# Sparse attention and GELU layers on one core: an earlier request for the last batch's queries and keys, and new instruction orders in five of eight halves

## The chip, the cores and the metric

The kernel runs on one core of a Trainium2 chip. The metric is the device time of one execution in microseconds (us). Five engines run in parallel, each through its own list of instructions in order: TensorE (PE for its matmuls, PEld for its weight loads), VectorE (DVE), ScalarE (ACT), GpSimd (POOL), and SyncE (SP), which here only issues transfers. Semaphores let one engine wait for another.

## The reference

Block-sparse attention on 4 batches of 8 heads with 768 tokens of 64 values, and then two layers with an exact GELU between them. A block is 32 tokens; a block of queries sees itself, its neighbours, the first and the last block, and three sampled blocks. The first and last block of queries see everything.

```
scores = scale * np.matmul(q, k.transpose(0, 1, 3, 2))
mask = np.abs(blk_i - blk_j) <= window
mask = mask | (blk_i == 0) | (blk_j == 0) | (blk_i == n_blocks - 1) | (blk_j == n_blocks - 1)
for qb in range(n_blocks):
    for kb in sampled_blocks[qb]:
        mask[qb * block:(qb + 1) * block, kb * block:(kb + 1) * block] = True
...
attn = np.exp(scores)
attn = attn / (np.sum(attn, axis=-1, keepdims=True) + 1e-09)
return np.matmul(attn, v).astype(np.float32)
...
h = x @ w_in
g = 0.5 * h * (1.0 + erf(h * inv_sqrt2))
return (g @ w_out).astype(np.float32)
```

x is the attention's output as 3072 rows of 512; w_in is 512 x 2048 and w_out 2048 x 512.

## The kernel before, in words

**Halves.** Each batch is worked in two halves of 384 tokens (`units`, L336), eight in all. The first half of a batch is dense: it also holds the two blocks of queries that see everything. The second is not. For each half, in order, comes its attention, then its first layer, and then its second layer, which is mixed into the attention of the next half.

**The attention of a half** works in rounds. A round is a score tile in PSUM, of two blocks of queries (four activations) or, in a dense round, of one of the two full blocks for half of the heads. `scores` (L347) makes the products on TensorE, `maxima` (L376) the negated row maxima on DVE (`nm`), `exponentials` (L389) the exponentials on ACT (`pp`), and `turned` (L408) transposes them on DVE (`pT`, or `ptd` for a dense round). When the rounds of a group are through, `values` (L429) makes the products with the values on TensorE (`av`; L442 is the dense one of 96 products, L481 the others of 104, or 92 for a group of three blocks), `divided` (L491) divides on DVE (`den`, `rec`, `xh`), and `outputs` (L508) turns the result on TensorE (`tx`) and copies it with ACT into `xT`, the first layer's input. PSUM has three score-sized tiles (`psA`), which scores, values and the first layer share, and two single banks that the second layer's sums and the turns use in alternation.

**The first layer** (`ffn1_step`, L547) is 64 products from `xT` (`hp`, L536), and ACT's GELU of them (`g`). **The second layer** (`ffn2_pieces`, L572) is 48 products (`op`, L579) in three sums of 16, each then copied by ACT (`os`, L563) and stored by SP (L565).

**The order of the work** is written out by hand. `manual_schedule` (L58) leaves each engine's list as the program writes it, and `attention` (L612) writes a half by a string of words, `PLANS` (L744): `s`, `m`, `e`, `t` with a number are scores, maximum, exponential and transpose of that round; `w`, `d`, `o` with a letter are values, division and output of a group (`d` the dense one; `O` copies the output in two pieces); `f` with a number is that many of the second layer's products; `S` asks for finished sums to be stored; `G` loads ACT's table for the GELU; `x` calls a function by name. Since each engine has its own list, a word places an instruction only among those of the same engine. The second half of a batch also holds, as its last two rounds, the first two dense rounds of the next batch (`ahead`), so that in the fourth half s6 and m6 belong to the third batch's first dense round. That half's words put s7 and m7 ahead of s6 and m6.

**Queries and keys.** From the third batch on they come by token: `load_by_token` (L123) issues six transfers of 128 KB from POOL for the queries into `qn`, and six for the keys into `kn`. Then `turn_queries` (L135) has SP issue one transposing transfer from `qn` into the batch's turned queries, and `turn_keys` (L132) one from `kn` a half later. POOL and SP take what they issue in order. `hold_loads` (L170) is a copy of one element on POOL (`mark`, L172) that waits for the value that it reads: what stands behind it on POOL isn't issued earlier. In the loop over the halves (L765), before the change, the hold and the loads of both the third and the fourth batch stand behind the first step of a first layer (L784 to L789). For the fourth, the last, that is the first layer of the fourth half, and the value held on is the half's second output copy in `xT`. Behind these loads on POOL stand another hold and the copies of sampled blocks into `gb` (L807, L808) for the fifth half.

Of the kernel before, what the change touches and what calls it, by code (L numbers as in the profile page):

```python
# [20 lines left out]
def kernel(  # L21
# [12 lines left out]
    B, H, S, D = q.shape  # L34
# [42 lines left out]
    kn = const.tile([P, H, PI * D], BF16, name="kn")  # L77
    qn = const.tile([P, H, PI * D], BF16, name="qn")
# [91 lines left out]
    def hold_loads(x):  # L170

        nc.gpsimd.tensor_copy(mark, x)  # L172
# [166 lines left out]
    column = {}  # L339
    for n, unit in enumerate(units):  # L340
        for t, quad in enumerate(unit.quads):
            for i in range(4):
                column[unit.b, 4 * quad + i] = (xTs[n % 2], P * t + BL * i)

    st = {}

    def scores(unit, *rnds):  # L347
# [28 lines left out]
    def maxima(rnd):  # L376
        A = st[rnd, "A"]
        nm = small.tile([P, 4], F32, name="nm")
        if rnd[0] == "s":
            n = len(rnd[1])  # L380
            A4 = A.rearrange("p (g j c) -> p g j c", g=2, j=2)
            nc.vector.tensor_reduce(out=nm[:, 0:2 * n].rearrange("p (g j) -> p g j", g=2),  # L382
                                    in_=A4[:, :, 0:n, :], op=ALU.max, axis=AX.X, negate=True)
        else:
            nc.vector.tensor_reduce(out=nm[:, 0:1], in_=A[:, 0:S], op=ALU.max, axis=AX.X,  # L385
                                    negate=True)
        st[rnd, "nm"] = nm

    def exponentials(rnd):  # L389
        A, nm = st.pop((rnd, "A")), st.pop((rnd, "nm"))  # L390
# [349 lines left out]
    def next_keys(b):  # L740
# [22 lines left out]
    }  # L763

    for n, unit in enumerate(units):  # L765
        nxt = units[n + 1] if n + 1 < len(units) else None
        b = unit.b
# [9 lines left out]
        for s in range(KOUT // 2):  # L777
            ffn1_step(n, 2 * s)
            if s == 0:
                if n == 0:  # L780
                    hold_loads(sampled(nxt.place[J1[7]], NR - 1)[0:1, BW - 1:BW])
                    gather(nxt, J1[8:], others, engine=nc.gpsimd)
                    ones(1)
                elif fresh and b + 2 < B:  # L784
                    xT, t0 = column[b, unit.groups[-2][0]]
                    hold_loads(xT[0:1, 0, t0:t0 + 1])
                    load_by_token(qn, q, b + 2)
                    load_by_token(kn, k, b + 2)
                    turn_queries(b + 2)  # L789
                elif nxt is not None and not fresh:  # L790
                    if b + 1 < B:
                        turn_keys()
                        hold_loads(sampled(nxt.place[J1[7]], NR - 1)[0:1, BW - 1:BW])
                        load_values(b + 1)
                    else:
                        gather(nxt, J1[8:], others, engine=nc.gpsimd)
            if s == 7 and nxt is not None:
                table(AF.Exp)
                if n > 0 and not fresh and b + 1 < B:
                    next_keys(b + 1)  # L800
                    hold_loads(keys(b + 1)[0:1, NB, 0:1])
                    gather(nxt, J1[8:], others, engine=nc.gpsimd)
            if fresh and s == 0:
                gather_fixed(keys(b + 1), nxt.place)
                gather(nxt, J0[3:9], known)
                gather(nxt, J0[:3], known)
                hold_loads(sampled(nxt.place[J0[2]], NR - 1)[0:1, BW - 1:BW])  # L807
                gather(nxt, J0[9:], others, engine=nc.gpsimd)  # L808
        filler = ffn2_pieces(n)
# [8 lines left out]
            attention(nxt, filler, PLANS[1], extra | {"v": later_values, "s": partial(spare_key, keys(1))},  # L818
                      ahead=units[n + 2])
        else:  # L820
            attention(nxt, filler, PLANS[n + 1], ahead=units[n + 2] if not fresh and b + 1 < B else None)


# [28 lines left out]
```

## Time and profile before

| | us |
|---|---|
| median of 3 runs | 274.39 (273.89 to 275.86) |
| the profiled execution | 274.32 |
| its span, first to last instruction | 272.5 |
| TensorE busy in the span | 252.6 |
| attention of the third to eighth half (with the second layer of the half before) | 19.67, 17.77, 21.56, 17.86, 19.44, 17.15 |
| the first layer between them | 10.4 each |

The granted clock of TensorE was 1.00 throughout. The chain of work that ended last runs for 82% of the span through PE and for 7% through ACT. In the views, a line of the timeline gives start, length, engine, source line and operation, out<-in and the number of instructions merged; in brackets stands the idle time of that engine just before, with what ended it, where "issue" means that the profile shows nothing that the engine waited for. In the DMA views q0 holds the transfers that POOL issues, q1 those that SP issues, and q8 the fetching of instructions; the columns are packets, MB, and the time that the packets took as a share of 16 engines over the window.

### The profile page before, as it was taken

Reading aid. Unit: us, or ns where it says so; the run is one execution under the profiler, and the core shown is the slowest. Engines: PE = TensorE matmul, PEld = TensorE weight load, DVE = VectorE, ACT = ScalarE, POOL = GpSimd, SP = SyncE. Lnnn points to the kernel's source line nnn. Section 1 sums busy time; section 2 is a strip of 40 time slices with the busy share of each in tenths; the row PEclk is TensorE's granted clock in tenths of the full one; section 3 lists DMA queues with packets and bytes.
Section 4 is the critical chain, followed back from the end, with each engine's and each line's share of the span. In section 5 each row is a group of like instructions: output and inputs, shape, how many; then the busy total and the mean of one; then the engine's idle time right before and its main releaser. Section 6 shows DMA issues by size and latency. Waiting matters only on the chain.

```text
span 272.5 us, 11555 instructions
## 1 busy us (share of the span) xinstructions
PE 252.6 (93%) x4944; PEld 144.1 (53%) x4944; DVE 203.3 (75%) x472; ACT 206.7 (76%) x381; POOL 103.6 (38%) x212
## 2 busy tenths in 40 slices
PE   0899679999999999999999799999999999999994
PEld 0634455455664656545554466455655655465543
DVE  7499659599897988699989686698869892981000
ACT  8789655977869975897779755995889956986611
POOL 7799960735964000940991002920040160000000
PEclk9999999999999999999999999999999999999999
DMA  6999399979999117921999017911101110021012
GB/s 96 186 191 149 55 147 202 206 123 143 93 172 129 43 41 158 104 28 68 98 156 172 8 41 156 117 43 44 38 1 43 43 41 0 5 79 41 0 38 82
DMA packets 75910, 24.41 MB, mean 90 GB/s; under 512 B 65489, under 2 KB 72914, under 8 KB 75858
## 3 DMA queue, kind: packets, MB, share of 16 engines
q0 software_dynamic: 57440, 13.64, 53.4%
q1 hardware_dynamic: 18418, 10.03, 15.5%
q8 instruction: 39, 0.64, 1.0%
q14 instruction: 13, 0.11, 0.1%
HBM read 27.26 MB, written 6.29 MB: 123 GB/s over the span
## 4 chain that ended last, share of the span: by engine, by line
PE 82%; ACT 7%; issue 3%; DMA 3%; DVE 3%; POOL 1%; POOLq 0%; ACTq 0%
PE hp L536 30%; PE op L579 26%; PE av L481 10%; PE sc L356 6%; DMA qn<-in_q_dram 3%; PE tx L513 2%; PE op L608 2%; ACT pp L399 2%; PE av L442 2%; PE pt L241 2%; ACT pp L403 2%; PE av L608 1%; DVE xh L501 1%; ACT L427 1%; ACT gb L295 1%
## 5 line engine op out<-in xcount | busy, mean ns | idle before, releaser
L536 PE MATMUL hp<-xT,w_in_sb 128*128 128x384 bf16 (+2 forms) x536 | 85.1, 319 | 1.4 <-issue 1.4
L579 PE MATMUL op<-w_out_sb,g 128*128 128x512 bf16 x336 | 83.4, 380 | 0.4 <-issue 0.4
L399 ACT ACTIVATE pp<-sc,nm 128x256 bf16<-128x256 f32 x176 | 74.2, 544 | 4.4 <-DVE nm L382 3.8
L536 PEld LDWEIGHTS <-w_in_sb 128*128 128x128 bf16 x536 | 51.2, 98 | 34.5 <-issue 1.5
L558 ACT ACTIVATE g<-hp 128x768 bf16<-128x768 f32 x56 | 45.1, 809 | 25.6 <-PE hp L536 25.6
L382 DVE TENSOR_REDUCE nm<-sc 128x4 f32<-128x1024 f32 (+1 forms) x48 | 53.0, 1119 | 12.3 <-PE sc L356 11.9
L579 PEld LDWEIGHTS <-g 128*128 128x128 bf16 x336 | 29.4, 98 | 33.9 <-issue 6.0
L316 DVE COPY gb<-kv 128x392 bf16 x177 | 35.8, 282 | 0.0
L416 DVE STREAM_TRANSPOSE pT<-pp 128x512 f32<-128x512 f32 (+1 forms) x48 | 30.6, 652 | 2.8 <-ACT pp L399 2.6
L172 POOL COPY mark<-gb 1x1 bf16<-1x1 bf16 x6 | 1.1, 179 | 80.9 <-DVE gb L316 80.9
L316 POOL COPY gb<-kv 128x392 bf16 x54 | 26.3, 537 | 14.1 <-PE av L481 13.8
L481 PEld LDWEIGHTS <-pT 64*32 64x32 bf16 (+1 forms) x2400 | 25.5, 91 | 7.3 <-issue 2.1
L481 PE MATMUL av<-kv,pT 64*32 64x130 bf16 (+1 forms) x1344 | 27.4, 221 | 1.7 <-issue 0.9
L521 ACT COPY xT<-tx 128x512 bf16<-128x512 bf16 (+3 forms) x34 | 13.7, 432 | 14.0 <-PE tx L513 14.0
L148 POOL DMA_DIRECT2D kv<-in_v_dram x32 | 23.0, 727 | 2.4 <-issue 2.4
L356 PE MATMUL sc<-gb,qT 64*32 64x256 bf16 x704 | 18.1, 273 | 2.2 <-issue 1.5
L356 PEld LDWEIGHTS <-qT 64*32 64x32 bf16 x832 | 9.9, 90 | 18.1 <-issue 10.0
L427 ACT ACT_TABLE_LOAD x15 | 19.2, 1283 | 0.3
L501 DVE TENSOR_TENSOR xh<-av,rec 128x512 bf16<-128x512 f32 (+2 forms) x28 | 18.2, 652 | 1.0
L385 DVE TENSOR_REDUCE nm<-sc 128x1 f32<-128x768 f32 x16 | 14.8, 949 | 4.6 <-PE sc L356 4.6
L403 ACT ACTIVATE pp<-sc,nm 128x768 bf16<-128x768 f32 x16 | 17.0, 1106 | 1.2 <-DVE nm L385 0.9
L481 PE MATMUL av<-gb,pT 64*32 64x130 bf16 x924 | 17.3, 222 | 0.5 <-issue 0.5
(80 smaller groups left out, 247.2 us busy)
## 6 DMA issues: line engine op xcount, KB each, us to landing
out_dram<-os SPq DMA_DIRECT2D x23, 256.0 KB, 2.1
kv<-in_v_dram POOLq DMA_DIRECT2D x32, 96.0 KB, 3.3
w_in_sb<-in_moe_w_in_dram POOLq DMA_DIRECT2D x4, 512.0 KB, 7.1
w_out_sb<-in_moe_w_out_dram POOLq DMA_DIRECT2D x2, 1024.0 KB, 13.5
kn<-in_k_dram POOLq DMA_DIRECT2D x4, 384.0 KB, 11.4
qn<-in_q_dram POOLq DMA_DIRECT2D x4, 384.0 KB, 12.7
qn<-in_q_dram POOLq DMA_DIRECT2D x12, 128.0 KB, 4.9
kn<-in_k_dram POOLq DMA_DIRECT2D x12, 128.0 KB, 5.3
```

Of the source, the lines that this page charges most:

```text
L148: nc.gpsimd.dma_start(out=kvs[b % 2][32 * hh:32 * hh + 32, 0:NB, c0:c0 + D], in_=v[b, h].rearrange("(n p) d -> p n d", p=BL))
L316: (engine or nc.vector).tensor_copy(to[:, None, :], src[:, bass.ds(at[j][r], 1), :])
L356: nc.tensor.matmul(o, lhsT=qT[rows, j // 4, pr, BL * (j % 4):BL * (j % 4) + BL], rhs=rhs(rows, pr), start=True, stop=True)
L382: nc.vector.tensor_reduce(out=nm[:, 0:2 * n].rearrange("p (g j) -> p g j", g=2), in_=A4[:, :, 0:n, :], op=ALU.max, axis=AX.X, negate=True)
L399: nc.scalar.activation(at[:, x // n, x % n], A[:, a:a + 256].rearrange("p (e c k) -> p e c k", e=2, k=BL), AF.Exp, bias=nm[:, x:x + 1])
L403: nc.scalar.activation(pp[:, 0:S].rearrange("p (c k e) -> p c e k", e=2, k=BL), A[:, 0:S].rearrange("p (c e k) -> p c e k", e=2, k=BL), AF ...
L416: nc.vector.transpose(pt.rearrange("p g c x -> p (g c) x")[:, :, 64 * s:64 * (s + n)].bitcast(F32), pp[:, 0:512 * n].bitcast(F32).rearrang ...
L427: nc.scalar.activation(junk, zero[0:1, 0:1], func)
L481: nc.tensor.matmul(av[32 * s:32 * (s + w), h, VS * G:VS * G + V2], lhsT=pv[rows, G, c % 4, BL * s:BL * (s + w), c // 4], rhs=src[rows], st ...
L536: nc.tensor.matmul(hp[:, i, c0:c1], lhsT=w_in_sb[:, ki, (m + i) * P:(m + i + 1) * P], rhs=xTs[n % 2][:, ki, c0:c1], start=(ki == 0), stop= ...
L558: nc.scalar.activation(g[:, m:m + 2, 0:T], hp[:, :, 0:T], AF.Gelu)
L579: nc.tensor.matmul(op, lhsT=g[:, m, t * P:(t + 1) * P], rhs=w_out_sb[:, m, :], start=(m == 0), stop=(m == KOUT - 1))
```

## The change

**The loads.** A function `later_batch` holds and then issues the twelve loads. For the third batch it is called where the loads stood before. For the fourth, it is called by a new word `xl` behind m6 in the fourth half's string, and the hold reads that maximum (`nm`), which is kept under a name of its own for this. `turn_queries` stays where it was, behind the first step of the first layer. The other words of the fourth half are the same.

**The orders.** The strings of the third, fifth, sixth, seventh and eighth half (2, 4, 5, 6, 7 in `PLANS`) hold the same work in another order; some output copies go in two pieces that went in one, and the reverse (two ACT copies fewer in all). Of the strings the diff shows the fourth half's changed line and the first lines of the fifth and sixth half's:

```diff
+    def later_batch(b, x):
+        hold_loads(x)
+        load_by_token(qn, q, b)
+        load_by_token(kn, k, b)
...
-        st[rnd, "nm"] = nm
+        st[rnd, "nm"] = st["nm"] = nm
...
-            "f2 da f2 s5 m5 f1 t4 e7 f2 S e5 s6 m6 t5 wb S e6 oa f1 db t6 wc f1 ob dc f4 t7 oc G f1"),
-        4: ("f1 s2 m2 s1 s0 f7 m1 f2 m0 S e2 t2 e1 f1 e0 f2 s3 f2 m3 f2 t1 f1 S f1 s4 s5 f2 t0 m4 f1 e3 f2 m5 "
-            "e4 f2 wd t3 s6 f3 dd m6 t4 e5 od f3 s7 e6 m7 e7 wa da f8 G t6 f1 oa t7 t5 wc wb dc oc f4 db Ob "
...
-        5: ("s2 s3 m2 f1 S f2 m3 f3 e2 f1 t2 f1 e3 f5 s0 s1 f4 m0 f6 m1 e0 f1 S t3 f3 s4 wb e1 f2 m4 f1 e4 f4 "
...
+            "f2 da f2 s5 m5 f1 t4 e7 f2 S e5 s6 m6 xl t5 wb S e6 oa f1 db t6 wc f1 ob dc f4 t7 oc G f1"),
+        4: ("s2 s1 m2 s0 f6 m0 S e2 f1 m1 f4 e1 f1 s3 f4 e0 f2 t2 f1 m3 f2 t1 t0 s4 wd e3 s5 f2 m4 e4 dd f3 "
+            "od m5 t3 s6 f2 m6 e5 f1 wa t4 s7 m7 f3 e6 f1 da f1 t5 f2 e7 f2 t6 f1 Oa wb t7 G db wc dc f1 Ob "
...
+        5: ("f1 s2 s3 s0 f4 m2 f2 m3 f1 e2 f2 e3 f1 m0 f6 s1 t2 f2 e0 S f1 t3 f2 m1 wb f2 db f1 s5 f3 t0 f1 "
...
                 elif fresh and b + 2 < B:
-                    xT, t0 = column[b, unit.groups[-2][0]]
-                    hold_loads(xT[0:1, 0, t0:t0 + 1])
-                    load_by_token(qn, q, b + 2)
-                    load_by_token(kn, k, b + 2)
+                    if b == 0:
+                        xT, t0 = column[b, unit.groups[-2][0]]
+                        later_batch(b + 2, xT[0:1, 0, t0:t0 + 1])
                     turn_queries(b + 2)
...
-            attention(nxt, filler, PLANS[n + 1], ahead=units[n + 2] if not fresh and b + 1 < B else None)
+            def batch_after():
+                later_batch(b + 2, st["nm"][0:1, 0:1])
+            attention(nxt, filler, PLANS[n + 1], {"l": batch_after},
+                      ahead=units[n + 2] if not fresh and b + 1 < B else None)
```

Lines below the new function are numbered 5 higher in the changed program, so that L382 of before is L387 there.

POOL, around the last batch's loads, before (`mark` is the hold's element, `kv` the batch's keys and values, `qn` and `kn` the queries and keys by token):

```order
L316 COPY gb<-kv_84 128x392
L172 COPY mark<-xT_92 1x1
L126 DMA qn<-in_q_dram 128x8x64 x6
L126 DMA kn<-in_k_dram 128x8x64 x6
L172 COPY mark<-gb 1x1
```

And in the changed program:

```order
L316 COPY gb<-kv_84 128x392
L172 CAST mark<-nm 1x1
L126 DMA qn<-in_q_dram 128x8x64 x6
L126 DMA kn<-in_k_dram 128x8x64 x6
L172 COPY mark<-gb 1x1
```

On POOL nothing has moved; the hold ahead of the loads reads the fourth half's maximum and not its output.

DVE in the fifth half, from the first sparse transpose to the dense division's end, before (`nm` a maximum, `pT` and `ptd` transposes, `den`, `rec`, `xh` the division):

```order
L416 STREAM_TRANSPOSE pT<-pp 128x8x64
L382 TENSOR_REDUCE nm<-sc 128x4
L421 STREAM_TRANSPOSE ptd<-pp 128x12x32 x2
L382 TENSOR_REDUCE nm<-sc 128x4 x2
L416 STREAM_TRANSPOSE pT<-pp 128x8x64
L496 TENSOR_SCALAR den<-av 128x2x2
L499 RECIPROCAL rec<-den 128x2x2
L501 TENSOR_TENSOR xh<-av,rec 128x2x128
```

And in the changed program:

```order
L421 STREAM_TRANSPOSE pT<-pp 128x8x64
L387 TENSOR_REDUCE nm<-sc 128x4
L426 STREAM_TRANSPOSE ptd<-pp 128x12x32 x2
L387 TENSOR_REDUCE nm<-sc 128x4
L501 TENSOR_SCALAR den<-av 128x2x2
L504 RECIPROCAL rec<-den 128x2x2
L506 TENSOR_TENSOR xh<-av,rec 128x2x128
```

One maximum and one transpose that stood ahead of the dense division now stand behind it.

ACT at the end of the eighth half, from the last exponentials to the last output copy, before (`pp` the exponentials, `xT` the output copies, ACT_TABLE_LOAD the GELU's table):

```order
L399 ACTIVATE pp<-sc,nm 128x2x4x32 x4
L521 COPY xT_92<-tx 128x2x128 x2
L427 ACT_TABLE_LOAD
L427 ACTIVATE junk<-zero 1x1
L521 COPY xT_92<-tx 128x2x96 x2
L521 COPY xT_92<-tx 128x2x128 x2
```

And in the changed program:

```order
L404 ACTIVATE pp<-sc,nm 128x2x4x32 x4
L432 ACT_TABLE_LOAD
L432 ACTIVATE junk<-zero 1x1
L526 COPY xT_92<-tx 128x4x128 x2
L526 COPY xT_92<-tx 128x4x96
```

The table load stands ahead of all three output copies, and each copy is one instruction.

20 rows, old and new, of the table PLANS are left out of this document.

## The prediction

> **What bounds the kernel now.** I read the page's busy times first, then the busy times stage by stage (each window is one half's attention on TensorE, with the 48 output products of the half before mixed in), then the chain of work that ended last.
>
> ```profile
> PE 252.6 (93%) x4944; PEld 144.1 (53%) x4944; DVE 203.3 (75%) x472; ACT 206.7 (76%) x381; POOL 103.6 (38%) x212
> ...
> q8 instruction: 39, 0.64, 1.0%
> ```
> ```profile
> 82.71:102.38 19.67, 19.54 (x565) 10.81 (x562) 17.56 (x31) 17.73 (x38) 2.42 (x6) 1.00 0.45 68
> 112.78:130.55 17.77, 17.77 (x466) 9.29 (x466) 16.43 (x27) 15.68 (x33) 6.99 (x15) 1.00 0.52 60
> 140.95:162.51 21.56, 19.55 (x563) 10.78 (x563) 17.46 (x31) 17.20 (x37) 3.23 (x8) 1.00 0.71 86
> 172.91:190.77 17.86, 17.73 (x467) 9.45 (x467) 15.16 (x24) 14.82 (x33) 6.18 (x13) 1.00 0.53 62
> 201.18:220.62 19.44, 19.21 (x563) 10.80 (x563) 17.72 (x30) 17.34 (x37) 5.66 (x12) 1.00 0.08 30
> 231.02:248.17 17.15, 16.73 (x451) 9.03 (x449) 13.05 (x21) 15.26 (x35) 0.00 (x0) 1.00 0.10 34
> ```
>
> Columns: length, then busy time of PE, PEld, DVE, ACT and POOL. The rows are the third to the eighth half. TensorE is busy for nearly all of each; length less PE is idle time: 0.13, 0.00, 2.01, 0.13, 0.23 and 0.42 us. The five stages dealt anew hold 2.92 us of it and the fifth half 2.01 of that; the fifth is 2.1 us longer than the seventh, which does the same work. No reordering of equal work can win much more than these 2.92 us: 1.1% of the run. The chain of work that ended last says where the fifth half's idle time lies:
>
> ```profile
> 144.73 0.34 PE sc L356 x16
> 145.07 1.40 PE op L579 x6
> 146.47 0.56 PE sc L356 x32
> 147.03 1.62 PE op L579 x7
> 148.65 1.25 PE av L442 x78
> 149.91 1.48 issue
> 151.38 0.47 PE av L442 x18
> 151.85 0.34 PE sc L356 x16
> 152.20 0.75 PE op L579 x3
> 152.95 0.12 PE tx L513 x2
> 153.07 0.65 PE op L579 x3
> 153.72 0.23 PE sc L356 x8
> 153.95 0.70 PE av L481 x78
> 154.65 0.46 issue
> 155.11 0.68 PE av L481 x24
> ```
>
> TensorE stops twice, 1.48 and 0.46 us, and both stops fall inside a run of equal products whose inputs were there ("issue": no wait that the profile shows). Between the ends of the two stops stand 18+16+3+2+3+8+78 = 128 products. Each is a weight load and a matmul, so exactly 256 instructions, and the page's q8 moves 0.64 MB in 39 packets, 16.4 KB each: 64 bytes for each of 256 instructions. So I read both stops as TensorE waiting for its next block of instructions. The DMA views of four short windows bear this out (144.8 to 148.9, two rows; then 148.9 to 149.0, 152.4 to 152.5 and 126.9 to 127.1, one each):
>
> ```profile
> q1 hardware_dynamic: 1919, 0.52, 101.6%
> q0 software_dynamic: 986, 0.12, 46.9%
> ```
> ```profile
> q8 instruction: 1, 0.02, 59.6%
> ```
> ```profile
> q8 instruction: 1, 0.02, 75.8%
> ```
> ```profile
> q8 instruction: 1, 0.02, 32.9%
> ```
>
> A packet's time is its share times 16 engines times the window: 0.95, 1.21 and 1.05 us. The block begun in 148.9 to 149.0 lands at about 149.9, and TensorE goes on 1.48 us later; the one begun in 152.4 to 152.5 lands at 153.6, and TensorE goes on 1.47 us later. Undisturbed, the loop is: ask when TensorE enters the block before (151.38), start 1.05 us later, 1.2 us of packet, 1.47 us until it runs: 3.73 us per 256 instructions. The block of the first stop was asked for 128 products before it (78+7+32+6 and the last 5 of the 16 scores: about 144.9) and started only after 4.05 us. From 144.8 to 148.9 no q8 packet started, while q1 was full with the transposition of the last batch's queries. That transfer is what the change moves. [...]
>
> **The change part by part.** *The loads.* In the profiled run:
>
> ```profile
> 129.36 0.30 POOL L172 COPY mark<-xT 1x1 bf16<-1x1 bf16 x1 [10.55 <-ACT xT L521]
> 129.89 6.06 POOL L126 DMA_DIRECT2D qn<-in_q_dram  x6 [0.23 <-issue]
> 135.94 5.34 POOL L126 DMA_DIRECT2D kn<-in_k_dram  x6
> 141.28 0.18 POOL L172 COPY mark<-gb 1x1 bf16<-1x1 bf16 x1
> ```
> ```profile
> 125.44 0.92 DVE L385 TENSOR_REDUCE nm<-sc 128x1 f32<-128x768 f32 x1
> ```
> ```profile
> 140.29 5.48 SPq L136 DMA_TRANSPOSE qT<-qn  x1
> ```
>
> The holding copy now waits for the maximum that ends at 126.36 (the seventh in number, the last of that half in time). With the 0.53 us that lay between copy and first issue, and 0.13 us from a release to the copy, the loads begin at 126.36+0.13+0.53 = 127.0, 2.87 us earlier. All twelve issues move with it, 11.4 us in all, and then the copies into gb behind them. POOL is free from the copies before until then (the 10.55 us wait in the first row), so the wait added there holds nobody else: behind it stand only these loads. On SP the transposition keeps its place; it begins when the queries have landed, so at 137.4 and not 140.29, and the block of instructions that queued behind it starts at about 148.95-2.87 = 146.1 and can run at 146.1+0.95+1.48 = 148.5.
>
> *The fifth half.* Where is that block needed? Before, it began with product 185 after the half's first stage ended, at 149.91, 8.96 us into the half. In the new order those 184 products hold 21 output products, not 26, the whole 96 dense value products, not 78, and 67 score products, not 80: 5 x 0.231 (7 in 1.62) earlier, 18 x 0.016 later, 13 x 0.0175 (32 in 0.56) earlier, so 7.85 us in, at 148.8. That is 0.3 us after 148.5. Bounds: 1.48 us gained if the block comes in time; 0 if it still waits for the transposition to its old end. It is nearer the first: I take 1.4. The second stop: the next 256 instructions hold 8 output products against 6, so 2 x 0.231 more work fills the loop; bounds 0 and 0.46, taken 0.36 for 0.1 left over.
>
> *The orders on DVE and ACT.* In the dense halves DVE (17.5 of 19.6) and ACT are nearly as full as TensorE, so an order that makes either late shows at once. Chained from the durations of these rows, the new orders of the third and seventh half leave the products ready when TensorE comes; I take 0 for both, between -0.36 (their idle time, 0.13 and 0.23, gone) and +0.6 (each late once by a maximum's half).
>
> *The sixth half.* Its block boundaries fall differently: between two of them now stand 15 score, 8 output and about 104 value products: 0.27+1.85+0.94 (78 in 0.70) = 3.06, some 3.4 with what each change of kind cost above (0.1 three times), against a loop of 3.73. So a stop of up to 0.4, or 0 if a quicker loop serves it; I take 0.2 lost.
>
> *The eighth half.*
>
> ```profile
> 244.75 1.28 ACT L427 ACT_TABLE_LOAD   x1
> ...
> 246.15 0.50 ACT L521 COPY xT<-tx 128x192 bf16<-128x192 bf16 x2
> ```
> ```profile
> 246.71 0.38 PE tx L513 x4
> ```
>
> The table load stood ahead of an output copy, whose bank the last turn on TensorE then waited for (the idle 0.42 us of the eighth half). Now the table is loaded ahead of all three copies, while TensorE still makes values, so that wait goes; but the last divisions stand behind more transposes on DVE. Bounds 0 to 0.42 gained; I take 0.3.
>
> *The fourth half* keeps its order. The moved loads reach into its last 3.5 us. Its last block packet started in 126.9 to 127.1 and took 1.05, so it landed at 128.05. Before, the window from the first issue, 129.89 to 130.95, has this one row of a queue and no data packet:
>
> ```profile
> q8 instruction: 1, 0.02, 6.7%
> ```
>
> From issue to data it took at least 1.06 us, so the new loads' first packets come after about 128.1. I take 0, between 0 and the 3.0 us that the block behind the transposition was late.
>
> Sum: -1.4 -0.36 -0.3 +0.2 = -1.86. The profiled run took 274.32 us around its span of 272.5 (1.82 outside), and the median of the runs is 274.39, so no correction is needed: 274.32-1.86 = 272.46, said as **272.4 us**.
>
> **The rivals.** *A: the stop stays.* The transposition is only 2.87 us earlier and the margin 0.3 us: if it spreads out among the key loads, the block starts as late as now; or the stops are no block waits at all. Then only the eighth half and the sixth are left: 274.32-0.3+0.2 = 274.2. For it speaks the small margin; against it that the block started as soon as q1 thinned out. [...]
>
> *B, slower: the stop moves into the fourth half.* Its last block is used with hardly any slack (128.05+1.48 = 129.53, and the stage ends at 130.55). If the load packets come before that packet, and hold it as q1 held the other, the 3.0 us are paid there, from the point at which data packets start before 127.0; the fifth half's gain remains: 274.32+3.0-1.86 = 275.5. Against it: the issues can't start before 126.36.
>
> *C: all idle time goes.* 274.32-2.92 = 271.4. For it: the new orders have no worse count of changes of kind. Against it: the stop that the sixth half may gain.
>
> *D: denser runs.* The new orders meet the 3.73 us loop, or a late DVE, in the third, sixth and seventh half: 0.4 twice in the sixth and 0.4 in each other, 1.6 us, less the 1.86 and the 0.2 already taken for the sixth: 273.9. For it: the count in the sixth half; against it: in the other halves I count 3.5 to 3.9 us of work per block.
>
> **How the numbers follow.** Forecast 0.47, A 0.15, B 0.10, C 0.13, D 0.15. The likeliest alone spans 271.7 to 273.1 (its own bounds, 0.7 to either side). The range for 8 in 10 reaches from 271.2, just below C, to 275.0, beyond A and D and short of most of B. 1% of the median is 2.7 us, about what a measurement of this kernel can tell from no change: under 271.65 lie most of C and a small part of the forecast, 0.17; over 277.1 only B with a longer hold, 0.05; the rest, 0.78, is within 1%.
>
> **What would show it.** In the changed profile: (1) the first query load issued at about 127 and the transposition at about 137.4; (2) the fifth half about 19.7 us long, with no wait of over 0.3 us inside its dense value products; (3) a q8 packet starting by about 146 and not at 149; (4) the fourth half still 17.8, and the sixth about 18.1; (5) no wait for an output copy ahead of the eighth half's last turn, and that half about 16.9. I am wrong if the stop is still there with the block already landed long before (then it was no block wait), if it is found again in the fourth half, or if DVE or ACT are named as what TensorE waits for in the new orders.

## The result and the profile after

| | us |
|---|---|
| before, median of 22 runs | 273.79 (272.21 to 276.97) |
| changed, median of 22 runs | 272.22 (271.03 to 273.93) |
| changed / before | 0.9948, 95% interval 0.9928 to 0.9967 |
| the profiled execution of the changed kernel, its span | 271.83, 270.0 |

The medians differ by 1.57 us (0.6%); the interval of the ratio, times 273.79, is 0.9 to 2.0 us. This is a small gain, inside the 1% within which the prediction placed it. In the profiles of the experiments whose granted clock was below 1.00 (named where they come), only the places and sizes of single stops are read, not the lengths of stages; e12's profile, at 0.992, is the exception.

The stage rows first (the profile after, by windows, columns as before: length, then busy time of PE, PEld, DVE, ACT and POOL):

```profile
82.26:101.54 19.28, 18.59 (x559) 10.84 (x562) 17.49 (x31) 16.34 (x37) 2.64 (x6) 1.00 0.37 73
111.94:129.71 17.77, 17.11 (x461) 9.25 (x465) 16.66 (x28) 15.65 (x33) 9.62 (x18) 1.00 0.65 68
140.11:159.83 19.72, 18.88 (x560) 10.91 (x564) 17.67 (x31) 17.63 (x39) 2.15 (x5) 1.00 0.42 74
170.23:188.23 18.00, 17.41 (x462) 9.22 (x466) 14.67 (x23) 14.67 (x32) 5.81 (x13) 1.00 0.51 59
198.64:218.30 19.66, 18.46 (x559) 10.50 (x564) 17.84 (x31) 16.43 (x36) 6.28 (x12) 1.00 0.09 30
228.70:245.86 17.16, 16.32 (x445) 9.00 (x449) 12.84 (x21) 14.99 (x32) 0.00 (x0) 1.00 0.09 33
```
```profile
PE 248.2 (92%) x4909; PEld 143.6 (53%) x4944; DVE 201.7 (75%) x472; ACT 205.6 (76%) x379; POOL 103.8 (38%) x212
```

The fifth half went from 21.56 to 19.72 us. The others changed by -0.39, 0.00, +0.14, +0.22 and +0.01. A warning on the second column: this profile holds 4909 matmul records where 4944 weight loads ran, so 35 are missing, and length less PE is no idle time here. Only the lengths are read.

Next the chain that ended last in the fifth half, the stretch where TensorE had stopped for 1.48 and 0.46 us:

```profile
146.63 1.53 PE av L447 x96
148.16 0.34 PE sc L361 x16
148.50 0.16 issue
148.66 1.03 PE op L584 x4
149.69 0.11 PE tx L518 x2
149.80 0.40 PE sc L361 x16
150.20 0.75 PE op L584 x3
150.95 1.27 PE av L486 x104
```

All 96 dense values and all 104 others now run without a break. The one "issue" row, 0.16 us ahead of an output product, is what one missing record of such a product leaves (0.21 to 0.26 us from one to the next here, and the fifth half's row has 560 matmul records for 564 weight loads), and I don't read it as a stop.

What had moved, on POOL, on SP's queue, and in the DMA view of 145.2 to 145.4 us:

```profile
125.66 0.18 POOL L172 CAST mark<-nm 1x1 bf16<-1x1 f32 x1 [7.81 <-DVE nm L390]
126.19 6.26 POOL L126 DMA_DIRECT2D qn<-in_q_dram  x6 [0.35 <-issue]
```
```profile
136.91 5.38 SPq L136 DMA_TRANSPOSE qT<-qn  x1
```
```profile
q8 instruction: 1, 0.02, 29.5%
```

The loads start with the maximum, the transposition follows, and the block of instructions that had waited until 149 starts at 145.3 and takes 0.295 x 16 x 0.2 = 0.94 us.

### The profile page after: what moved, and what is told of

It reads as the page before. It is cut to its first block, busy times and chain, and to the rows that moved or that the text cites. A ratio compares the mean times of both kernels' runs of the same rounds, so it can differ in the third digit from the quotient of the medians.

```text
span 270.0 us, 11525 instructions
## 1 busy us (share of the span) xinstructions
PE 248.2 (92%) x4909; PEld 143.6 (53%) x4944; DVE 201.7 (75%) x472; ACT 205.6 (76%) x379; POOL 103.8 (38%) x212
## 4 chain that ended last, share of the span: by engine, by line
PE 77%; ACT 9%; DVE 5%; issue 4%; DMA 3%; POOL 1%; POOLq 0%; ACTq 0%
PE hp L541 31%; PE op L584 23%; PE av L486 8%; PE sc L361 6%; ACT pp L404 3%; DMA qn<-in_q_dram 3%; ACT pp L408 2%; PE tx L518 2%; PE op L613 2%; PE pt L241 2%; PE av L447 2%; DVE pT L421 1%; DVE nm L387 1%; PE av L613 1%; DVE xh L506 1%
## 5 line engine op out<-in xcount | busy, mean ns | idle before, releaser
L584 PE MATMUL op<-w_out_sb,g 128*128 128x512 bf16 x302 | 75.5, 380 | 3.4 <-issue 2.3
L387 DVE TENSOR_REDUCE nm<-sc 128x4 f32<-128x1024 f32 (+1 forms) x48 | 52.9, 1115 | 13.9 <-PE sc L361 13.8
L432 ACT ACT_TABLE_LOAD x15 | 19.2, 1283 | 0.3
L568 ACT COPY os<-op 128x512 f32<-128x512 f32 (+1 forms) x23 | 13.2, 574 | 5.8 <-PE op L613 4.3
```

The source lines that it names most:

```text
L584: nc.tensor.matmul(op, lhsT=g[:, m, t * P:(t + 1) * P], rhs=w_out_sb[:, m, :], start=(m == 0), stop=(m == KOUT - 1))
```

## The experiments

Theory T, from the prediction: the two stops are TensorE waiting for its next block of 256 instructions, and the first block was late because the last batch's loads and transposition filled the DMA engines. Rival R1: they are not block waits, or the transfers don't matter, and the gain comes from the new orders. Rival R2 (B of the prediction): the transfers only choose which block is late, so that the same stop can come back in another half. No view shows when a block is asked for. As in the prediction I put the ask where TensorE enters the block before, an estimate: from there to the packet's start the profile before has 1.05 us at the second stop (151.38 to 152.43).

For stage lengths I use rounds: from the end of one first layer to the end of the next, that is, one half's attention and its first layer. The ends are those of the rows of 64 first-layer products in each run's chain of waits, which no missing record of another product moves. The rounds of the third to eighth half in us, all from profiles with a clock of 1.00 but e12's, 0.992:

| round | before | changed | e12, changed again | e1 loads alone | e2 orders alone | e3 turn late | e6 old fifth order | e8 no transposition |
|---|---|---|---|---|---|---|---|---|
| third | 30.07 | 29.68 | 29.68 | 30.07 | 29.68 | 30.08 | 29.70 | 30.07 |
| fourth | 28.17 | 28.17 | 28.17 | 28.41 | 28.44 | 28.17 | 28.40 | 28.40 |
| fifth | 31.96 | 30.12 | 30.12 | 29.95 | 31.25 | 29.85 | 29.94 | 29.84 |
| sixth | 28.27 | 28.41 | 28.11 | 28.26 | 28.12 | 29.75 | 28.11 | 28.25 |
| seventh | 29.84 | 30.06 | 29.68 | 29.84 | 29.68 | 29.84 | 29.86 | 29.85 |
| eighth | 27.55 | 27.56 | 27.34 | 27.55 | 27.38 | 27.55 | 27.38 | 27.55 |

The second and third profile are of one kernel: they agree to 0.01 us in the third to fifth round and differ by 0.2 to 0.4 in the later ones. Differences of 0.4 in a single profile are therefore not read there, nor are the 0.2 to 0.3 of the fourth round, which come and go with the same order of products.

**e1 and e2: the two parts alone.** e1 is the kernel before with the change's code for the loads and this line, all other strings as before:

```diff
-            "f2 da f2 s5 m5 f1 t4 e7 f2 S e5 s6 m6 t5 wb S e6 oa f1 db t6 wc f1 ob dc f4 t7 oc G f1"),
+            "f2 da f2 s5 m5 f1 t4 e7 f2 S e5 s6 m6 xl t5 wb S e6 oa f1 db t6 wc f1 ob dc f4 t7 oc G f1"),
```

e2 is the changed kernel with that line's `xl` taken out again and the loads where they had been:

```diff
-                    if b == 0:
+                    if True:
                         xT, t0 = column[b, unit.groups[-2][0]]
                         later_batch(b + 2, xT[0:1, 0, t0:t0 + 1])
```

> The kernel before with the last batch's loads moved to the fourth half's seventh maximum, and all orders as before. Theory (TensorE waits for a block of 256 instructions that queues behind the queries' transposition): the transposition starts 2.9 us earlier, the block can run at about 148.5 on the clock of the run before, and it is needed at 149.9, so the 1.48 us stop in the dense value products goes; the second stop of 0.46 us stays, since the 128 products between hold 3.27 us of work against a loop of 3.73. Fifth half 20.0 to 20.2 us instead of 21.56, all other halves as before, time 1.5 us under before (ratio 0.9945). Rival (the new orders shorten the half, the loads don't matter): fifth half 21.5, time as before.

> The changed kernel with the last batch's loads back behind the first step of the fourth half's first layer. Theory: the block still starts only when the transposition is through, about 150.5 on this program's clock until it can run, and the new order needs it at about 148.1, so a stop of about 2.4 us stands just behind the 96 dense value products (one to three score products behind them): fifth half about 22 us, time 0.5 us above the kernel before at most 1 us below it (ratio 0.998 to 1.002). Rival (the orders do it): fifth half 19.7, time as the changed kernel, ratio 0.995.

Measured: e1 272.91 us, ratio 0.9954 (0.9927 to 0.9980); e2 274.24, ratio 1.0005 (0.9974 to 1.0037). The loads alone bring what the whole change brings (0.9948); the orders alone bring nothing that shows in the time, though their interval leaves room for 0.7 us, and e2's profile, one of its faster executions at 273.29 us, has six rounds that are 1.3 us shorter in all. So the gain as measured doesn't come from the orders, as R1 has it. In e1 neither stop is left, the second one included, which I had expected to stay. This is the row of e1's chain of waits at the old place of the second stop, all 104 products in one piece:

```profile
152.81 1.26 PE av L486 x104
```

And e2 shows the stop where the new order's count puts it, behind 96 dense values and 2 scores (chain of waits of e2, then its DMA view from 146.1 to 147.7 us):

```profile
147.68 1.51 PE av L447 x96
149.19 0.21 PE sc L361 x2
149.40 0.98 issue
150.38 0.41 PE sc L361 x14
```
```profile
q1 hardware_dynamic: 1815, 0.46, 127.6%
```

The place is as counted, the size 0.98 and not the 2.4 expected, and the fifth half took 20.85 us (31.25 less 10.40), not 22. The window holds q1 alone, without one packet of q0 or q8. Counted back 128 products, the block was asked for at about 145.2 and, with 1.05 us from ask to start, would have started at about 146.2; it started in 147.7 to 147.9, just as q1 emptied (51.8% there): here the transposition by itself held a block, by this estimate for about 1.5 us.

**e8 and e3: the suspect transfer.** e8 is the kernel before without the last batch's transposition of queries, so that batch is computed with an older batch's queries; the loads stay. e3 is the kernel before with that transposition a half later, behind the keys'. Both have this edit of the kernel before:

```diff
-                    turn_queries(b + 2)
+                    if b == 0:
+                        turn_queries(b + 2)
```

and e3 also this:

```diff
                         turn_keys()
+                        if n == 4:
+                            turn_queries(b + 1)
```

> The kernel before with the transposition of the last batch's queries left out (that batch then takes the queries that stood in the buffer), loads and orders as before. Theory: this is the whole price of the transposition: both stops of the fifth half go, 19.2 instead of 21.6, the sixth half unchanged at 17.8; ratio 0.993 to 0.995, as the changed kernel or a little under. Rival (the twelve loads, or something else in the fifth half, make the stop): fifth half 21.5, ratio 1.0.

> The kernel before, with loads and orders as they were, but the transposition of the last batch's queries issued one half later, behind that of its keys. Theory: with q1 empty between 144.8 and 148.9 the block starts about 1.1 us after it is asked for, in spite of the loads, so the 1.48 us stop goes; the second stop of 0.46 stays: fifth half 20.0 to 20.2; the sixth half may gain up to 0.5 us, because the transposition now runs into its start. Time about 1.2 us under before (ratio 0.9955). Rival 1 (the twelve loads on q0 hold the block): fifth half still 21.5. Rival 2 (no wait for instructions at all, but for the dense values' inputs): fifth half still 21.5.

Measured: e8 273.54, ratio 0.9981 (0.9953 to 1.0009); e3 274.49, ratio 1.0014 (0.9985 to 1.0043). Both stops left the fifth half in both kernels (rounds 29.84 and 29.85 against 31.96), with the loads and the orders as before; for e3 I had expected the second to stay. That settles the cause of the stops: the transposition. But e8's time fell by 1.0 us only by the medians, and by 0.5 us by the ratio, whose interval reaches past 1; 0.993 to 0.995 was expected. Its six rounds are 1.9 us shorter in the profile, which has 0.2 us more ahead of them and 0.5 more behind. Why is not settled.

In e3 the time didn't fall at all, and the chain of waits of e3 in the sixth half shows where it went:

```profile
177.66 0.81 PE av L481 x91
178.47 0.80 issue
179.27 0.58 PE av L481 x13
...
182.22 0.80 PE av L481 x80
183.03 0.47 issue
183.49 0.58 PE av L481 x14
```

Two stops of the old shape, each in a run of equal values, 1.27 us together, and the sixth round is 1.5 longer. I had expected 0.5 at most. The DMA view of e3 from 174.5 to 178.4 has this row:

```profile
q0 software_dynamic: 1958, 0.24, 155.8%
```

That is not the moved transposition, issued at 165.24 behind the keys' at 161.04, but the loads of the last batch's values on q0, which are issued from 166.12 on and were still running. So in e3 the stop of 0.80 us came behind q0's loads, as the one of 1.48 before came behind q1's transposition; that the transposition had pushed these loads back is likely, but was not taken apart.

**e4, e5 and e9: are they blocks of 256 instructions?** If so, adding or leaving out instructions early moves every boundary. e4 adds 16 idle products (32 instructions) in the first half; e5 makes 16 products of the third half's first layer twice (32 instructions as well); e9 leaves out 16 idle products. e4's edit of the kernel before (e9 has 16 in place of 48), and then e5's:

```diff
-    attention(units[0], idle_products(32),
+    attention(units[0], idle_products(48),
```
```diff
+            if n == 2 and m < 4:
+                ffn1_products(hp, n, m, i, 0, T)
             ffn1_products(hp, n, m, i, covered.pop((m, i), 0), T)
```

> The kernel before with 16 more idle products (32 instructions) on TensorE in the first half, nothing else. Theory: block boundaries lie at fixed counts of instructions, so in the fifth half both stops fall 16 products earlier: behind 62 of the 96 dense value products, not 78, and behind 62 of the 104 sparse ones, not 78; their sizes change by no more than the work moved across (0.3 us). Rival (a wait for data, or for another engine): both stops stay behind 78. The time itself is a few us longer by the added products in the first half and says nothing.

> The kernel before with 16 products of the third half's first layer made twice (32 instructions more, some 2.6 us), well ahead of the fourth half, so that the loads, the transposition and the fifth half keep their distances. Theory: block boundaries lie at fixed counts of instructions, so the first stop falls behind 62 of the 96 dense value products instead of 78, still over 1 us long; a second stop, if there, behind 62 of the next 104. Rival (a wait for data or another engine): behind 78 as before, or at another place that isn't 16 products earlier.

> The kernel before with 16 idle products of the first half taken away (32 instructions fewer), nothing else. The shift by 32 the other way gave new stops in four halves. Theory (blocks of 256 instructions, 3.7 us from asking for one to running it): the boundaries now fall 32 instructions later in the work. Counted from the order, three blocks then hold far less than 3.7 us of work: in the third half 2 output, 8 score, 104 value and 14 score products, 2.2 us; in the fourth 1 output, 16 score, 104 value and 6 score products, 1.9 us; in the seventh 16 score, 96 dense value and 14 score products, 2.3 us. So stops of 1.4, 1.8 and 1.4 us, each inside the run of scores at the block's end, and less than 0.5 us in some others: time 3 to 6 us over before in spite of less work, ratio 1.011 to 1.022. Rival (placement of blocks doesn't matter, or only behind a transfer): time as before or under it, ratio 0.995 to 1.0.

Measured, one run each of e4 and e5: 283.52 (clock 0.986) and 280.61 us (clock 1.00); e9 274.16, the median of 10 runs, ratio 0.9995 (0.9969 to 1.0022), its profile at 0.981. Neither e4 nor e5 has a stop behind 62 products, as was expected of both: the two old stops are gone there. The block of the first one now starts 4.8 us (e4) and 5.6 us (e5) into the fifth half, against 8.0 before; it is asked for 16 products sooner, but that this is the whole reason is not shown. Four new stops stand in the fourth, fifth, seventh and eighth half. Two of them in e5's chain of waits:

```profile
129.24 0.96 PE av L481 x83
130.20 1.39 issue
131.59 0.24 PE av L481 x5
...
248.58 1.30 PE av L481 x103
249.88 1.63 issue
```

The others took 1.02 and 1.58 us. In e4 the same four halves stop for 1.37, 1.51, 1.36 and 1.89, at the same products. Two unlike edits, in different halves, with nothing in common but 32 instructions more, give the same four stops: the boundaries here lie at fixed counts of instructions. At each new stop a block held only 1.8 to 2.1 us of work, by my count, against the loop of 3.73.

e9 shows the shift itself. Its order of work in the fifth half is that of before, with 16 products fewer far ahead, and both old stops fall 16 products later, behind 94 and 94 where they had been behind 78 and 78 (chain of waits of e9):

```profile
149.09 1.48 PE av L442 x94
150.57 1.18 issue
...
154.10 0.83 PE av L481 x94
154.93 0.56 issue
```

e9 also gives one stop counted ahead of the run, behind 14 scores of the third half (chain of waits of e9):

```profile
92.56 1.19 PE av L481 x104
93.74 0.34 PE sc L356 x14
94.08 0.99 issue
95.07 0.28 PE sc L356 x2
```

and two that were counted and did not come, 1.8 us in the fourth half and 1.4 in the seventh; the 3 to 6 us that I expected were wrong. In the fourth half the packet had started at 118.6, while TensorE was still amid 12 output products that the profile lists from 117.84 to 120.60, ahead of the boundary I had counted from. So here the packet started before TensorE reached that boundary, with slow products ahead of it (0.23 us each). The count gave the places of the stops; for their sizes it was an upper bound in e9.

**e7: the loads earlier still.** Rival B says that this brings the stop into the fourth half. Meanwhile I doubted it, since I took the token loads on q0 to hold a block for 0.4 us at most, which no run had shown. Against the changed kernel:

```diff
-        3: ("f1 s3 s1 m3 s0 f5 m1 e3 f2 e1 f2 m0 t3 e0 f6 s2 m2 e2 f3 t1 f5 t0 f4 s4 m4 t2 wa s7 f1 m7 f2 e4 "
-            "f2 da f2 s5 m5 f1 t4 e7 f2 S e5 s6 m6 xl t5 wb S e6 oa f1 db t6 wc f1 ob dc f4 t7 oc G f1"),
+        3: ("f1 s3 s1 m3 s0 f5 m1 e3 f2 e1 f2 m0 t3 e0 f6 s2 m2 e2 f3 t1 f5 t0 f4 s4 m4 xl t2 wa s7 f1 m7 f2 e4 "
+            "f2 da f2 s5 m5 f1 t4 e7 f2 S e5 s6 m6 t5 wb S e6 oa f1 db t6 wc f1 ob dc f4 t7 oc G f1"),
```

> The changed kernel with the loads behind the fourth half's fifth maximum (m4), some 7 us earlier, so that their packets run beside the last two or three instruction blocks of the fourth half. Theory (the transposition on q1 holds a block for as long as its descriptors are queued, the by-token loads on q0 cost it 0.4 us at most): fourth half 17.5 to 18.0, fifth as in the changed kernel, ratio 0.995. Rival B of the prediction (the loads hold a block in the fourth half as the transposition did in the fifth): a stop of 1 to 3 us in the fourth half, 18.5 to 20.5, ratio 1.0 to 1.006.

Measured: 275.37, ratio 1.0027 (0.9992 to 1.0061), where the changed kernel has 0.9948 and, in e12, 0.9940: some 0.8% or 2.2 us lost. TensorE's timeline in e7, then its DMA views from 127.4 to 130.7 and from 130.7 to 130.8 (clock 0.988; this execution took 278.12 us, and behind the stop its first layer took 11.57 us instead of 10.40, so only the stop itself is read):

```profile
130.06 1.03 PE L584 MATMUL op<-w_out_sb,g 128*128 128x512 bf16 x4
134.11 0.33 PE L518 MATMUL tx<-identity,xh 96*128 96x96 bf16 x4 [3.02 <-DVE gb L308]
```
```profile
q0 software_dynamic: 2674, 0.34, 160.6%
```
```profile
q8 instruction: 1, 0.02, 108.1%
```

A stop of 3.02 us in the fourth half, at the last turn. No instruction packet starts from 127.4 to 130.7, while q0 is full of the token loads; the one that then comes takes 1.081 x 16 x 0.1 = 1.73 us, lands at about 132.5, and 1.6 us later TensorE goes on. It came through while q0 was still full, with 1151 packets from 131 to 132, so this block did not wait until the queue was empty. The releaser in brackets misleads: the copy into `gb` that it names is no input of a turn, and in the changed kernel the same turn starts at 128.52, with those copies only at 130.54. My doubt fell, and R2 holds: the loads by token held a block too, with a stop of 3.02 us here against 1.48 behind the transposition.

**e6, e10, e11 and e12: is there something better?** e6 is the changed kernel with the fifth half's old order, since e1's fifth round (29.95) was shorter than the changed one (30.12). e10 has 4 idle products (8 instructions) fewer in the first half, e11 both edits, and e12 is the changed kernel again on the chip of e9 to e11. The first lines of e6's edit of the changed kernel, and then e10's:

```diff
-        4: ("s2 s1 m2 s0 f6 m0 S e2 f1 m1 f4 e1 f1 s3 f4 e0 f2 t2 f1 m3 f2 t1 t0 s4 wd e3 s5 f2 m4 e4 dd f3 "
+        4: ("f1 s2 m2 s1 s0 f7 m1 f2 m0 S e2 t2 e1 f1 e0 f2 s3 f2 m3 f2 t1 f1 S f1 s4 s5 f2 t0 m4 f1 e3 f2 m5 "
```
```diff
-    attention(units[0], idle_products(32),
+    attention(units[0], idle_products(28),
```

> The changed kernel with the fifth half's order of before; loads early, the other four orders new. The two profiles with that order and no stop had a fifth half of 19.2 us, the changed kernel 19.6. If that holds, fifth half 19.2, time 0.4 us under the changed kernel, ratio to before 0.9935. Rival (the new order of the fifth half carries a part of the gain): fifth half 19.7 or more, ratio 0.995 or above.

> The changed kernel with 4 idle products of the first half taken away (8 instructions fewer). Theory: counted from the order, the blocks with less than 3.6 us of work lack 0.84 us in all in the changed kernel and 0.21 us here, so 0.6 us less: ratio to before about 0.9925, 0.002 under the changed kernel's in this call. Rival (boundaries as they stand cost nothing in the changed kernel): no difference from it.

> The changed kernel with the fifth half's order of before, and 4 idle products fewer. Theory: the counts lack 0.42 us, 0.4 less than the changed kernel, and the fifth half may be 0.1 us shorter: ratio about 0.9925. Rival: as the changed kernel.

> The changed kernel itself, beside the three others on the same chip, as the measure for which of them beats it: ratio to before 0.993 to 0.997.

| | median us | ratio to before | 95% interval |
|---|---|---|---|
| e6 | 272.09 | 0.9925 | 0.9894 to 0.9955 |
| e10 | 271.93 | 0.9916 | 0.9885 to 0.9947 |
| e11 | 271.57 | 0.9920 | 0.9892 to 0.9948 |
| e12 | 272.54 | 0.9940 | 0.9920 to 0.9960 |

The four intervals overlap: none is shown to beat the change, though all three variants have lower medians than e12. e12 repeats the result (0.9940 against 0.9948). The fifth round is 0.18 us shorter with the old order in e6 (29.94 against 30.12), not the 0.4 expected: less its first layer it is 19.5 us, about as in e1 and e3, and not 19.2. Each order has a wait of its own. The rows are from TensorE's timeline, after the change and in e6:

```profile
157.51 0.40 PE L518 MATMUL tx<-identity,xh 128*128 128x128 bf16 x4 [0.36 <-DVE xh L506]
```
```profile
150.26 0.41 PE L361 MATMUL sc<-gb,qT 64*32 64x256 bf16 x16 [0.23 <-DVE den L501]
```

The new order divides a group late on DVE, and its turn waits 0.36 us; in e6 no wait of over 0.1 us stands ahead of that half's last turns, but scores behind the dense values wait 0.23 for DVE. The difference, 0.13, is most of the 0.18. e6's other rounds are not all as short as e12's, so its total is open.

## Why the prediction came out right, and where it did not

The forecast was 272.4 us against a median of 272.22, with the case that it called likeliest. Its sum was -1.86 us; the six rounds of the profile after are 1.86 shorter (175.86 to 174.00), and the medians differ by 1.57. That the first two figures are the same is luck: e12's profile of the same kernel is 2.76 shorter, and in the profile after the third half's 0.39, put at 0, stands against 0.14 and 0.22 lost in the sixth and seventh and an eighth that gained nothing. The main term was right, and not every other one.

**The reading of the bound** held. "TensorE waiting for its next block of instructions" was inferred from 128 products between two stops and from q8; e5 and e4 (same four stops from 32 instructions), e2 and e9 (stops at counted places, the two old ones 16 products on) and e8 (no transposition, no stop) now show it. Where queues were full, one crossing from block to block cost 0.98 (e2), 1.48 (before) and 3.02 us (e7). The reading reaches further than the prediction took it. The first half, which it didn't look at, stops three times (chain of waits before):

```profile
29.64 1.52 issue
...
34.33 0.65 issue
...
40.10 1.35 issue
```

At each a q8 packet lands 1.3 to 1.4 us before TensorE goes on, much as at the other stops. In the profile after they are 1.79, 0.37 and 1.35: these 3.5 us, more than the 1.94 that the change took out, are still there. What would shorten them was not tried.

**The first stop, -1.4, and the second, -0.36:** the fifth half and its round became 1.84 us shorter, against 1.76 predicted. The steps, one by one: loads at 127.0, found 126.19; transposition at 137.4, found 136.91; packet by 146.1, found about 145.3; its landing, 146.2, plus the 1.48 us until it can run is about 147.7, against 148.5. The program was itself 0.84 us earlier when the half began (140.11 against 140.95), so relative to that the steps fit to 0.4 us. The block was needed at about 148.2, so the margin was some 0.5 us, not 0.3. The sum hid errors of opposite sign: the 0.1 us left to each of the two stops is not there (1.94 went, not 1.76), and the half's late division costs 0.36, which the prediction had not looked for in this half. 1.94 less 0.36 is 1.58; which rows hold the other 0.26 is open. The second stop needed no new order either: it is gone in e1. I had treated it as a stop of its own; with the first gone, the second goes with it.

**The eighth half, -0.3:** mis-sized. The chain of waits after still runs through the table load:

```profile
239.25 1.72 ACT pp L404 x4
...
240.99 1.28 ACT L432
...
242.49 0.47 ACT xT L526
242.96 0.04 issue
243.00 0.38 PE tx L518 x4
```

The load (1.28 us) no longer stands between two output copies, but it stands ahead of the first, behind the last exponentials; TensorE still waits at the next turn, though only about 0.1 us. The half is 17.16 against 17.15 in the profile after, not about 16.9, so the fifth sign that the prediction named did not come there; its round is 0.17 to 0.21 shorter in e2, e6 and e12, which have the same order. "That wait goes" was too simple: the 1.28 us instruction, moved along an ACT that is busy for 14.99 of the half's 17.16 us, stands ahead of the next copy that TensorE waits for.

**The sixth half, +0.2:** 0.14 longer by its row, but its round is 28.11 in e12, 28.12 in e2 and 28.11 in e6 against 28.25 to 28.27 with the old order. There is no stop; the loop of 3.73 was an upper bound, as e9 shows, and the stop's term was 0.

**The third and seventh half, 0:** the third gained 0.37 to 0.40 in every profile of the table with the new order (29.68 to 29.70 against 30.07 to 30.08), where the prediction bounded it by the half's idle time, 0.13. So length less busy time was no bound on what an order can win: the whole half is now 19.28 us long, less than the 19.54 that TensorE had been busy in it before. Why was not taken apart. The seventh is within the scatter.

**The fourth half, 0, with rival B at 3.0:** it kept 17.77 us. The rival was priced right and closer than its chance of 0.10 says: in e7 the loads begin at 124.15, not 126.19, in a program that at that place runs 2.5 us later (its last maximum at 127.11, not 124.59), so 4.5 us earlier in the half (7 had been expected), and 3.02 us are lost there. Rival A (the stop stays) and R1 are refuted by e1 and e8; rival C's gain of 2.92 did not come by the medians, and D's losses in the third, sixth and seventh half did not come either; a late division did, but in the fifth.

**Open:** why e8 saves only 0.5 to 1.0 us in all; what made the first block start sooner in e4 and e5; whether it was the moved transposition that put e3's value loads ahead of the sixth half's block; whether e10 or e11 is faster than the change. The first and the last of these lie under 0.5% of the time, where two profiles of one kernel already differ by 0.9 us over six rounds.

## What to carry to other kernels

When a run of equal products breaks off with an "issue" gap, count the products to the next such gap and look when the instruction queue's packet started. Here the gaps stood 128 products apart; where the packet started 4.05 us after the estimated ask and not 1.05 (before), a transfer stood ahead of the fetch, and the remedy was to move that transfer, not the products. Around two of e4's stops the DMA share was 0.03: no queue was full there, and the block before was used up, in 1.8 to 2.1 us by my count, faster than the next came in the loop of 3.73. Place bursts of small packets between two fetches, where slow products keep these apart: after the change the packets of the transposition run from about 140 to 145, and with the slow products of the first layer before them (64 in 10.40 us) no block started between 130.7 and 145.3. A burst moved a few microseconds can give the stop to another half (e7: 4.5 us earlier in the half, a stop of 3.02 us in the fourth), so look at what every block boundary near the new place would meet. An edit of 32 instructions moved the boundaries behind it in e4, e5 and e9, so judge such an edit by the whole run and not by the work that it adds.

## What the runs showed of the hardware

- A fetch of 256 instructions (one q8 packet of 16,384 bytes) took 0.88 to 1.31 us in the fifth half of the profiles before and after, and at the stops of the profile before and of e7 TensorE went on 1.3 to 1.6 us after it had landed. Products with the values (104 in about 1.27 us, with a weight load each) used instructions up faster than the loop of 3.73 us brought them, so stops came without a full queue: 1.37 and 1.36 us in e4, where the DMA share was 0.03 from 130 to 135 and from 222 to 226, and 0.65 us at 34.33 before, where the block's own packet (1.18 us) was the only one from 31.2 to 33.6.
- A fetch was held by what other queues had in work. With the ask put at the block before's start, an estimate, the packet came 3.0 us later than the undisturbed 1.05 with q1 at 101.6% and q0 at 46.9% (before), about 2.3 with q0 at 160.6% and q1 at 26.1% (e7), and about 1.5 with q1 alone at 127.6% (e2). One of q1's 1919 packets before, nearly all under 512 bytes, took 1.016 x 16 x 4.1 / 1919 = 0.035 us on average. How a queue of such packets makes a wait of this size was not shown.
- 32 more instructions cost far more than their work in e5. It is 6.1 us above its kernel before (280.61 against 274.54): 2.6 us for 16 products of the first layer (its third round, 32.66 against 30.07), 5.6 for four new stops, less 2.0 for the two that went, 6.2 together. Instructions left out, 32 in e9 and 8 in e10, showed no such cost (0.9995, and 0.9916 against 0.9940).
